# Loading keys and values as pairs with 64 KB rows, and moving the value products into the second key step

## The chip, the cores and the metric

The kernel runs on one core of a Trainium2 chip, with nothing else on the chip. The metric is the device time of one execution in microseconds; the kernel before takes 383.8 us. The profile's span is about 1.4 us shorter than the time.

Five engines work side by side: PE (matmuls), DVE (vector), ACT (activations), POOL and SP. SP issues the large loads, and at the end the one store, in a fixed order: where one load must wait, all that follow it wait too. Sixteen DMA engines move the data.

## The reference, cut to what matters

One token attends to a cache of 65536 positions; a gated mixer is computed beside it and both are blended.

```python
# Hq 32 query heads, Hkv 4 key/value heads, Sk 65536, Dh 128, D 1024, all bfloat16
q = (x @ wq)                               # wq 1024 x 4096
scores = q k^T * Dh ** -0.5                # k_cache 4 x 65536 x 128
o = softmax(scores) v                      # v_cache 4 x 65536 x 128
a = o @ wo                                 # wo 4096 x 1024
z = gelu(x @ w_in); ...; b = (z1 * g) @ w_out   # w_in 1024 x 3584, w_out 1792 x 1024
out = gate * a + (1 - gate) * b
```

There is one query position, so every byte of the caches and weights is read once for very little arithmetic. Together they are 162.0 MB.

## The kernel before

The code below is condensed; cuts are marked with dots. The caches are cut into 16 *units* of keys and 16 of values, 4 MB each: 128 partitions with a row of 32 KB (16384 bfloat16). On the chip there is room for five units: three places for keys, used in turn, and two behind them (offset `VB`) for value pairs and weights. `stream` is the list of loads in the order in which SP issues them. A load waits until the last reader of what lay in its place is done.

```python
SUB = 16384; KR = 3; VB = KR * SUB         # elements of a row; 3 key places, then 2 more

def load_k(n):  load([("k", n)], kv(A_k_cache, n), kring())          # next of the 3 places
def load_v2(n): load([("v", n), ("v", n + 1)], kv(A_v_cache, n, True), VB)

load([("wq", 0)], rows(A_wq, 0, 8), VB)
load_k(0); load_k(1)
load([("win", 0)], rows(B_w_in, 0, 8), VB)
load_k(2); load_k(3)
load([("wout", 0)], rows(B_w_out, 0, 14), VB)
for i in range(6):
    load_k(2 * i + 4); load_v2(2 * i); load_k(2 * i + 5)
load_v2(12)
# ... values 14, 15 in key places, then w_o in six pieces, the last three cut 4 + 2 + 2

def issue():
    # ... for the next load of the stream, once all that lay in its place is read:
    for c in range(0, w, SUB):             # a load of 64 KB rows goes out as two of 32 KB rows,
        m = min(SUB, w - c)                # each with its own wait and its own semaphore
        P("SP", lambda e, ...: e.dma_start(arena[:, o:o + m], src),
          w=[("slot", x) for x in grains(off + c, m)], dma="s%d" % grains(off + c, m)[0])
```

A *key step* of one unit is four transposes on DVE, each followed by eight matmuls on PE. The place of a unit is free after its fourth transpose.

```python
def k_piece(n, p):
    P("DVE", lambda e: e.transpose(ktb(i)..., sl[:, 4096 * p:4096 * (p + 1)]...),
      r=keys[2 * p:2 * p + 2], w=[("kt", i % NKT)])
    if p == 3:
        done(("k", n))                     # the place may be loaded again
    # ... 8 matmuls on PE

k_step(0)
k_step(1, evac=0, own=True)
mixer_piece()          # w_in's matmuls on PE, then a chain of some 20 small steps, most of them on DVE
k_step(2)
wout_piece()
k_step(3, evac=2)
for i in range(6):
    a = 2 * i + 4
    k_step(a, evac=a - 1, ..., pts=(2 * i, 2 * i + 1), own=True)
    pv_piece(2 * i)                        # value products of the pair
    pv_piece(2 * i + 1)
    # ...
    k_step(a + 1, late=g)
```

Of the kernel before, what the change touches and what calls it, by code (L numbers as in the profile page):

```python
# [131 lines left out]
def bass_gated_mix__gqa_block_cached__mixer_gmlp__decode_kernel(  # L132
# [19 lines left out]
    DO = A_wo.shape[1]  # L152
# [7 lines left out]
    NP = Sk // PK  # L160
# [124 lines left out]
    stream = []  # L285
    place = {}

    GRAN = 2048

    def load(keys, src, off):  # L290

        n = len(stream)
        w = src.shape[1]
        for i, key in enumerate(keys):
            place[key] = (n, off + i * (w // len(keys)), w // len(keys))
        stream.append((keys, off, src))

    def rows(w, i, c):

        return w[128 * c * i:128 * c * (i + 1), :].rearrange("(p c) n -> p (c n)", c=c)  # L300

    def kv(cache, n, both=False):

        g, u = divmod(n, NP)
        blk = cache[0, g, 2 * PK * (u // 2):2 * PK * (u // 2 + 1), :]
        if both:
            return blk.rearrange("(p x) d -> p (x d)", p=128)
        return blk.rearrange("(p h x) d -> p h (x d)", p=128, h=2)[:, u % 2, :]

    WQ_N = HQ * Dh  # L310
    VB = KR * SUB
    ring = [0]

    def kring():
        s = ring[0] % KR
        ring[0] += 1
        return s * SUB

    def load_k(n):
        load([("k", n)], kv(A_k_cache, n), kring())  # L320

    def load_v2(n):
        load([("v", n), ("v", n + 1)], kv(A_v_cache, n, True), VB)

    load([("wq", 0)], rows(A_wq, 0, 8), VB)
    load_k(0)
    load_k(1)
    load([("win", 0)], rows(B_w_in, 0, 8), VB)
    load_k(2)
    load_k(3)  # L330
    load([("wout", 0)], rows(B_w_out, 0, 14), VB)
    for i in range(6):
        load_k(2 * i + 4)
        load_v2(2 * i)
        load_k(2 * i + 5)
    load_v2(12)
    load([("v", 14)], kv(A_v_cache, 14), kring())
    load([("v", 15)], kv(A_v_cache, 15), kring())
    for i in range(3):
        load([("wo", i, 0)], rows(A_wo, i, 8), VB + 8 * DO * i)  # L340
    s3 = kring()
    for c0, c1 in [(0, 4), (4, 6), (6, 8)]:
        load([("wo", 3, c0)], rows(A_wo, 3, 8)[:, DO * c0:DO * c1], s3 + DO * c0)

    issued = [0]
    used = set()
# [2 lines left out]
    def grains(off, w):  # L349
        return list(range(off // GRAN, (off + w + GRAN - 1) // GRAN))  # L350

    def issue():

        while issued[0] < len(stream):
            n = issued[0]
            keys, off, src = stream[n]
            w = src.shape[1]
            gr = grains(off, w)
            if any(k not in used for x in gr if x in owner for k in owner[x]):
                return  # L360
            for x in gr:
                owner[x] = keys
            for c in range(0, w, SUB):
                m = min(SUB, w - c)
                P("SP", lambda e, o=OFF["RING"] + off + c, m=m, src=src[:, c:c + m]: e.dma_start(arena[:, o:o + m], src),  # L365
                  w=[("slot", x) for x in grains(off + c, m)], dma="s%d" % grains(off + c, m)[0])
            issued[0] += 1

    def use(key):
# [100 lines left out]
    def k_piece(n, p):  # L470
        if n % NP == 0 and p == 0:
            q_piece(n // NP)
        sl, keys = use(("k", n))
        i = nkt[0]
        nkt[0] += 1
        P("DVE", lambda e: e.transpose(ktb(i).bitcast(F32), sl[:, 4096 * p:4096 * (p + 1)].bitcast(F32)),  # L476
          r=keys[2 * p:2 * p + 2], w=[("kt", i % NKT)])
        if p == 3:
            done(("k", n))

        def f(e):
            for fe in range(4):
                f2, ev = fe // 2, fe % 2
                o = QP * fe + 24 - 8 * p
                for b in range(2):
                    ins = mm(e, b > 0, sc_ps(n)[:, 512 * b:512 * (b + 1)], qpad[:, o:o + 128],
                                   vw(ktb(i), 2048 * b + 64 * f2 + ev, [[128, 16], [2, 32]]),
                                   start=(p == 0 and fe == 0), stop=(p == 3 and fe == 3), skip_group_check=True)
            return ins
        P("PE", f, r=["qpad", ("kt", i % NKT)], w=[KSC(n)])  # L490

    def score_piece(n):
        P("DVE", lambda e: e.tensor_scalar(scs(n), sc_ps(n), 0.0, None, op0=ALU.add, op1=ALU.max,  # L493
                                           accum_out=maxc[:, n:n + 1]), w=[("sc", n % NSC), ("mx", n), KSC(n)])
# [18 lines left out]
    def pt_piece(n):  # L513
        P("DVE", lambda e: e.transpose(ptsb(n), psb), r=["psb"], w=[("ptsb", n % 2)])  # L514
# [17 lines left out]
    def out_first(g):  # L532
        P("DVE", lambda e: e.tensor_reduce(gcol(g, K_L), lp[:, NP * g:NP * (g + 1)], AXX, ALU.add),
          r=[("lp", NP * g + u) for u in range(NP)], w=[("l", g)])
        P("PE", lambda e: e.matmul(mb[:, 0:1], bm, gcol(g, K_L), start=True, stop=True),  # L535
          r=["bm", ("l", g)], w=["mb"])
# [84 lines left out]
    def wout_piece():  # L621
        sl, keys = use(("wout", 0))

        def f(e):
            for c in range(FC):
                j = c % 4
                for s in range(2):
                    o = DO * c + 512 * s
                    ins = mm(e, s > 0, ob[32 * j:32 * j + 1, 512 * s:512 * (s + 1)], yb[:, c:c + 1], sl[:, o:o + 512],
                             start=(c < 4), stop=(c >= FC - 4), tile_position=(0, 32 * j), skip_group_check=True)  # L630
            return ins
        P("PE", f, r=["yb"] + keys, w=["ob"])
        done(("wout", 0))
        part = scs(4)
        P("ACT", lambda e: e.activation(part[0:97, :], ob[0:97, :], ACTF.Copy), w=[("sc", 4), "ob"])

        def f(e):
            for q in range(4):
                ins = e.matmul(fb[32 * q:32 * q + 1, 0:QW], col(C_E4)[0:97, :], part[0:97, QW * q:QW * (q + 1)],
                               start=True, stop=False, tile_position=(0, 32 * q), skip_group_check=True)  # L640
            return ins
        P("PE", f, r=["e4", ("sc", 4)], w=["fb"])


    def k_step(n, evac=None, gmax=None, pts=(), own=False, late=None):

        for p in range(4):
            k_piece(n, p)
            if p == 0 and evac is not None:
                score_piece(evac)  # L650
                if gmax is not None:
                    max_first(gmax)
            if p == 1 and gmax is not None:
                max_second(gmax)
            if p == 1 and pts:
                exp_piece(pts[0])
            if p == 2 and pts:
                pt_piece(pts[0])
                exp_piece(pts[1])
            if p == 3 and pts:  # L660
                pt_piece(pts[1])
            if late is not None:
                (out_second, out_third, out_fourth, lambda g: None)[p](late)
        if own:
            score_piece(n)

    k_step(0)
    k_step(1, evac=0, own=True)
    mixer_piece()
    k_step(2)  # L670
    wout_piece()
    k_step(3, evac=2)
    for i in range(6):
        a = 2 * i + 4
        k_step(a, evac=a - 1, gmax=(a - 1) // NP if a % NP == 0 else None, pts=(2 * i, 2 * i + 1), own=True)
        pv_piece(2 * i)
        pv_piece(2 * i + 1)
        g = i // 2 if i % 2 == 1 else None
        if g is not None:
            out_first(g)  # L680
        k_step(a + 1, late=g)
    score_piece(15)
    max_first(3)
    max_second(3)
    for n in (12, 13):
        exp_piece(n)
        pt_piece(n)
    for n in (12, 13, 14, 15):
        pv_piece(n)
        if n < 14:  # L690
            exp_piece(n + 2)
            pt_piece(n + 2)
    out_first(3)
    out_second(3)
    out_third(3)
    out_fourth(3)


    for i, c0, c1 in [(0, 0, 8), (1, 0, 8), (2, 0, 8), (3, 0, 4), (3, 4, 6), (3, 6, 8)]:
        sl, keys = use(("wo", i, c0))  # L700

        def f(e, i=i, sl=sl, c0=c0, c1=c1):
            for c in range(c0, c1):
                for q in range(4):
                    o = DO * (c - c0) + QW * q
                    ins = e.matmul(fb[32 * q:32 * q + 1, 0:QW], ovec[:, 8 * i + c:8 * i + c + 1],  # L706
                                   sl[:, o:o + QW], start=False, stop=(i == 3 and c == 7),
                                   tile_position=(0, 32 * q), skip_group_check=True)
            return ins
        P("PE", f, r=[("ovec", i)] + keys, w=["fb"])  # L710
        done(("wo", i, c0))
# [34 lines left out]
```

## Time and profile before

| | before |
|---|---|
| median of 4 runs | 383.81 us (383.70 to 384.15) |
| span of the profile | 382.3 us |
| PE busy, DVE busy | 234.6 us, 211.7 us |
| DMA: share of 16 engines' time | 98.8% |

The first lines of the profile page say what bounds the kernel. "DMA" is the mean busy share of the 16 DMA engines in 40 equal slices of the span, in tenths; the line "q1" gives packets, megabytes, and the time of the packets as a share of 16 engines' span.

```profile
span 382.3 us, 2522 instructions
...
PE 234.6 (61%) x1375; PEld 56.9 (15%) x785; DVE 211.7 (55%) x229; ACT 25.3 (7%) x39; POOL 1.5 (0%) x8
...
DMA  9999999999999999999999999999999999999995
...
q1 hardware_dynamic: 6200, 162.01, 98.8%
```

The row of nines is the whole story of the kernel before: the DMA engines work from start to end, and the other engines have time to spare. The packet records of the trace give the detail: a 32 KB packet starts every 1213 ns on an engine, which is 432 GB/s for sixteen.

The second view is the timeline of SP, which shows when each load was issued (start in us, duration, engine, line, what is loaded; "x2" stands for two issues in a row, the duration then runs from the start of the first to the end of the last).

```profile
...
64.51 0.33 SPq L365 DMA_DIRECT2D arena<-in_B_w_out_dram  x1
64.88 0.43 SPq L365 DMA_DIRECT2D arena<-in_A_k_cache_dram  x1
89.59 0.81 SPq L365 DMA_DIRECT2D arena<-in_A_v_cache_dram  x2
...
309.28 8.77 SPq L365 DMA_DIRECT2D arena<-in_A_v_cache_dram  x4
...
```

Key 4 goes out at 64.88 us. The DMA engines reach it only when w_out is in, after 85 us.

The third view is the timeline of DVE around the mixer. In brackets is the time that the engine was idle before the instruction, and what ended the wait.

```profile
...
31.52 4.50 DVE L476 STREAM_TRANSPOSE arena<-arena 128x2048 f32<-128x2048 f32 x2 [0.90 <-DMA arena<-in_A_k_cache_dram]
...
64.51 1.09 DVE L588 COPY arena<-obt 128x896 f32<-128x896 f32 x1 [9.06 <-PE obt L248]
...
72.47 4.50 DVE L476 STREAM_TRANSPOSE arena<-arena 128x2048 f32<-128x2048 f32 x2
78.46 2.31 DVE L476 STREAM_TRANSPOSE arena<-arena 128x2048 f32<-128x2048 f32 x1 [1.50 <-PE scp L248]
80.93 4.51 DVE L476 STREAM_TRANSPOSE arena<-arena 128x2048 f32<-128x2048 f32 x2 [0.15 <-PE scp L248]
...
```

Key 0 starts at 31.52 us, as soon as it has landed. The mixer's chain on DVE runs from 64.51 to 72.47, then come the transposes of key 2; its fourth ends near 83.2 us.

### The profile page before, as it was taken

The numbers are of one execution on the slowest core, as the hardware profiler recorded it, in microseconds if no ns is written. First come the engines' busy times: TensorE is split into PE (matmuls) and PEld (weight loads), VectorE is DVE, ScalarE is ACT, GpSimd is POOL, SyncE is SP. The second block draws the span as 40 slices with busy tenths as digits, with TensorE's granted clock in tenths as the row PEclk, the third lists the DMA queues.
The fourth block names the chain that finished last, engine by engine and source line by source line (L and its number), as shares of the span: only waits on it lengthen the run. The fifth ranks groups of instructions, "written<-read, shape, count | busy, mean of one in ns | idle before, by whom it ended". The sixth has DMA issues, their size and how long they took to land.

```text
span 382.3 us, 2522 instructions
## 1 busy us (share of the span) xinstructions
PE 234.6 (61%) x1375; PEld 56.9 (15%) x785; DVE 211.7 (55%) x229; ACT 25.3 (7%) x39; POOL 1.5 (0%) x8
## 2 busy tenths in 40 slices
PE   0055754286687578545793777377938673849344
PEld 0011111111121111101120112012201121112121
DVE  6116952785781698067935980579448914842020
ACT  1000000102030001000210010001200100031000
POOL 1000000000000000000000000000000000000000
PEclk9996998689979599959898998786979988778695
DMA  9999999999999999999999999999999999999995
GB/s 384 439 435 425 423 417 435 439 436 433 439 425 418 432 430 439 439 432 432 429 420 429 435 439 434 429 435 426 422 432 437 435 432 429 439 425 420 423 425 220
DMA packets 6246, 162.16 MB, mean 424 GB/s; under 512 B 728, under 2 KB 732, under 8 KB 988
## 3 DMA queue, kind: packets, MB, share of 16 engines
q1 hardware_dynamic: 6200, 162.01, 98.8%
q8 instruction: 8, 0.13, 0.1%
q14 instruction: 2, 0.02, 0.0%
q10 hardware_dynamic: 36, 0.00, 0.0%
HBM read 162.01 MB, written 0.00 MB: 424 GB/s over the span
## 4 chain that ended last, share of the span: by engine, by line
DMA 61%; PE 19%; DVE 18%; SPq 1%; ACT 1%; issue 1%
DMA arena<-in_A_k_cache_dram 33%; DVE arena L476 13%; DMA arena<-in_B_w_in_dram 8%; DMA arena<-in_A_wo_dram 7%; DMA arena<-in_B_w_out_dram 6%; PE obt L246 6%; DMA arena<-in_A_wq_dram 6%; PE obt L248 5%; PE scp L246 4%; PE scp L248 4%; DVE arena L493 1%; SPq L365 1%; DVE arena L514 1%; DVE arena L464 1%; DVE arena L549 0%
## 5 line engine op out<-in xcount | busy, mean ns | idle before, releaser
L476 DVE STREAM_TRANSPOSE arena<-arena 128x2048 f32<-128x2048 f32 x64 | 145.5, 2295 | 84.5 <-DMA arena<-in_A_k_cache_dram 71.9
L246 PE MATMUL scp<-arena 128*128 128x512 bf16 x256 | 112.5, 439 | 83.4 <-DVE arena L476 61.0
L248 PE MATMUL scp<-arena 128*128 128x512 bf16 x256 | 111.0, 434 | 0.0
L246 PE MATMUL obt<-arena 128*64 128x512 bf16 (+2 forms) x334 | 64.6, 428 | 30.6 <-DMA arena<-in_A_v_cache_dram 12.4
L248 PE MATMUL obt<-arena 128*64 128x512 bf16 (+2 forms) x334 | 64.1, 424 | 0.0
L246 PEld LDWEIGHTS scp<-arena 128*128 128x128 bf16 x256 | 27.5, 107 | 192.2 <-DVE arena L476 93.8
L509 ACT ACTIVATE arena<-arena 128x1024 bf16<-128x1024 f32 x16 | 18.4, 1148 | 237.5 <-DVE arena L505 127.4
L246 PEld LDWEIGHTS obt<-arena 128*64 128x64 bf16 (+1 forms) x334 | 19.4, 116 | 86.6 <-issue 79.1
L493 DVE TENSOR_SCALAR_CACHE_REDUCE arena<-scp 128x1024 f32<-128x1024 f32 x16 | 19.3, 1205 | 9.3 <-PE scp L248 9.3
L514 DVE STREAM_TRANSPOSE arena<-arena 128x1024 bf16<-128x1024 bf16 x16 | 19.4, 1214 | 9.0 <-PE obt L248 6.4
L706 PE MATMUL fbt<-arena 128*1 128x256 bf16 x128 | 6.2, 339 | 5.9 <-DMA arena<-in_A_wo_dram 5.7
L539 DVE RECIPROCAL arena<-mbt 128x1 f32<-128x1 f32 x4 | 0.6, 139 | 14.0 <-PE mbt L535 14.0
L441 DVE CAST arena<-obt 97x1024 bf16<-97x1024 f32 x1 | 1.2, 1224 | 11.5 <-PE obt L248 11.5
L712 DVE CAST arena<-fbt 97x256 bf16<-97x256 f32 x1 | 0.4, 425 | 11.3 <-PE fbt L706 11.3
L588 DVE COPY arena<-obt 128x896 f32<-128x896 f32 x1 | 1.1, 1093 | 9.1 <-PE obt L248 9.1
L464 DVE COPY arena<-arena 32x32 bf16<-32x32 bf16 x16 | 2.7, 166 | 6.2 <-PE scp L248 6.0
L407 PE MATMUL scp<-arena 8*128 8x1 bf16 x8 | 0.6, 197 | 8.4 <-DVE arena L402 8.4
L706 PEld LDWEIGHTS fbt<-arena 128*1 128x1 bf16 x128 | 2.8, 93 | 8.8 <-DMA arena<-in_A_wo_dram 6.7
L595 ACT ACTIVATE arena<-arena 128x28 f32<-128x28 f32 x1 | 0.2, 226 | 52.4 <-DVE arena L594 52.4
L549 DVE SCALAR_TENSOR_TENSOR arena<-obt,arena 128x512 bf16<-128x512 f32 x4 | 3.0, 751 | 0.1
L601 PE MATMUL mbt<-arena 128*128 128x1 f32 x2 | 0.4, 260 | 4.3 <-DVE arena L600 4.3
L509 ACT ACTIVATION_READ_ACCUMULATOR arena<-arena 128x1 f32 x16 | 3.0, 186 | 0.0
(88 smaller groups left out, 47.0 us busy)
## 6 DMA issues: line engine op xcount, KB each, us to landing
arena<-in_A_k_cache_dram SPq DMA_DIRECT2D x16, 4096.0 KB, 38.4
arena<-in_A_v_cache_dram SPq DMA_DIRECT2D x16, 4096.0 KB, 31.1
arena<-in_A_wq_dram SPq DMA_DIRECT2D x2, 4096.0 KB, 16.8
arena<-in_A_wo_dram SPq DMA_DIRECT2D x3, 2048.0 KB, 22.6
arena<-in_B_w_in_dram SPq DMA_DIRECT2D x1, 4096.0 KB, 25.2
arena<-in_B_w_out_dram SPq DMA_DIRECT2D x1, 3584.0 KB, 23.1
arena<-in_B_w_in_dram SPq DMA_DIRECT2D x1, 3072.0 KB, 32.2
arena<-in_A_wo_dram SPq DMA_DIRECT2D x1, 1024.0 KB, 26.5
```

The lines of the kernel that those rows point to most:

```text
L246: return e.matmul(*a, **kw)
L248: one = e.matmul(*a, **kw).ins
L365: P("SP", lambda e, o=OFF["RING"] + off + c, m=m, src=src[:, c:c + m]: e.dma_start(arena[:, o:o + m], src), w=[("slot", x) for x in grains ...
L441: P("DVE", lambda e: e.tensor_copy(psb[0:97, :], ob[0:97, :]), w=["psb", "ob"])
L464: P("DVE", lambda e, pb=pb: e.tensor_copy(vw(qpad, 24 + 32 * pb, [[QP, 4], [1, 8]], 32 * pb, 32), vw(qall, 8 * g, [[32, 4], [1, 8]], 32 * ...
L476: P("DVE", lambda e: e.transpose(ktb(i).bitcast(F32), sl[:, 4096 * p:4096 * (p + 1)].bitcast(F32)), r=keys[2 * p:2 * p + 2], w=[("kt", i % ...
L493: P("DVE", lambda e: e.tensor_scalar(scs(n), sc_ps(n), 0.0, None, op0=ALU.add, op1=ALU.max, accum_out=maxc[:, n:n + 1]), w=[("sc", n % NSC ...
L509: P("ACT", lambda e: e.activation(psb, scs(n), ACTF.Exp, bias=gcol(n // NP, K_NB), scale=SCALE, accum_out=lp[:, n:n + 1]), r=[("sc", n % N ...
L514: P("DVE", lambda e: e.transpose(ptsb(n), psb), r=["psb"], w=[("ptsb", n % 2)])
L549: P("DVE", lambda e: e.scalar_tensor_tensor(osc, ob[:, 512:1024], gcol(g, K_FB), osc, op0=ALU.mult, op1=ALU.add), r=[("fh", g, 1), "psb"], ...
L588: P("DVE", lambda e: e.tensor_copy(vw(zr, 0, [[FB4, 2], [32, FC], [1, 32]]), vw(ob, 0, [[512, 2], [1, FC], [FC, 32]])), w=[KZR, "ob"])
L706: ins = e.matmul(fb[32 * q:32 * q + 1, 0:QW], ovec[:, 8 * i + c:8 * i + c + 1], sl[:, o:o + QW], start=False, stop=(i == 3 and c == 7), ti ...
```

## The change

The intent is fewer and longer packets. Where two units that lie side by side in the cache can also lie side by side on the chip, they are loaded as one load with rows of 64 KB. Keys now come in pairs where the three places allow it, and stream and places are laid out for that: the last values move to other places, and so does w_o. A load is no longer cut into two. The value products run inside the second key step, since all values of a pair now land at once. The last cut of w_o is finer (5 + 2 + 1 instead of 4 + 2 + 2).

```diff
-    GRAN = 2048
+    GRAN = 1024
...
+    def load_k2(n, slot):
+        load([("k", n), ("k", n + 1)], kv(A_k_cache, n, True), slot * SUB)
...
     load([("wq", 0)], rows(A_wq, 0, 8), VB)
-    load_k(0)
-    load_k(1)
+    load_k2(0, 0)
     load([("win", 0)], rows(B_w_in, 0, 8), VB)
-    load_k(2)
-    load_k(3)
+    load_k(2, 2)
+    load_k(3, 0)
     load([("wout", 0)], rows(B_w_out, 0, 14), VB)
     for i in range(6):
-        load_k(2 * i + 4)
-        load_v2(2 * i)
-        load_k(2 * i + 5)
-    load_v2(12)
-    load([("v", 14)], kv(A_v_cache, 14), kring())
-    load([("v", 15)], kv(A_v_cache, 15), kring())
+        a = 2 * i + 4
+        if i % 3 == 2:
+            load_k(a, 2)
+            load_k(a + 1, 0)
+        else:
+            load_k2(a, (1, 0)[i % 3])
+        load_v2(2 * i, VB)
+    load_v2(12, SUB)
+    load([("v", 14)], kv(A_v_cache, 14), VB)
+    load([("v", 15)], kv(A_v_cache, 15), VB + SUB)
...
-            for c in range(0, w, SUB):
-                m = min(SUB, w - c)
-                P("SP", ... one load of 32 KB rows, w=[("slot", x) for x in grains(off + c, m)], ...)
+            P("SP", lambda e, o=OFF["RING"] + off, w=w, src=src: e.dma_start(arena[:, o:o + w], src),
+              w=[("slot", x) for x in gr], dma="s%d" % gr[0])
...
     mixer_piece()
     k_step(2)
-    wout_piece()
     k_step(3, evac=2)
+    wout_piece()
     for i in range(6):
-        k_step(a, evac=a - 1, ..., pts=(2 * i, 2 * i + 1), own=True)
-        pv_piece(2 * i)
-        pv_piece(2 * i + 1)
-        k_step(a + 1, late=g)
+        k_step(a, evac=a - 1, ..., pts=(2 * i, 2 * i + 1))
+        k_step(a + 1, evac=a, mid=mid)     # mid: both pv_piece, between the 2nd and 3rd transpose
```

More of the change, by code (lines that the diff above doesn't have):

```diff
@@ L311, in bass_gated_mix__gqa_block_cached__mixer_gmlp__decode_kernel, with load_k, load_v2 @@
     VB = KR * SUB
-    ring = [0]
-    def kring():
-        s = ring[0] % KR
-        ring[0] += 1
-        return s * SUB
-    def load_k(n):
-        load([("k", n)], kv(A_k_cache, n), kring())
-    def load_v2(n):
-        load([("v", n), ("v", n + 1)], kv(A_v_cache, n, True), VB)
+    def load_k(n, slot):
+        load([("k", n)], kv(A_k_cache, n), slot * SUB)
+    def load_k2(n, slot):
+        load([("k", n), ("k", n + 1)], kv(A_k_cache, n, True), slot * SUB)
+    def load_v2(n, off):
+        load([("v", n), ("v", n + 1)], kv(A_v_cache, n, True), off)
     load([("wq", 0)], rows(A_wq, 0, 8), VB)
-    load_k(0)
-    load_k(1)
+    load_k2(0, 0)
     load([("win", 0)], rows(B_w_in, 0, 8), VB)
-    load_k(2)
-    load_k(3)
+    load_k(2, 2)
+    load_k(3, 0)
     load([("wout", 0)], rows(B_w_out, 0, 14), VB)
     for i in range(6):
-        load_k(2 * i + 4)
-        load_v2(2 * i)
-        load_k(2 * i + 5)
-    load_v2(12)
-    load([("v", 14)], kv(A_v_cache, 14), kring())
-    load([("v", 15)], kv(A_v_cache, 15), kring())
+        a = 2 * i + 4
[8 more added lines that the diff above has]
+    load([("v", 15)], kv(A_v_cache, 15), VB + SUB)
+    WO_AT = [0, 8 * DO, 16 * DO, 24 * DO]
+    WO_CUT = [(0, 5), (5, 7), (7, 8)]
     for i in range(3):
-        load([("wo", i, 0)], rows(A_wo, i, 8), VB + 8 * DO * i)
-    s3 = kring()
-    for c0, c1 in [(0, 4), (4, 6), (6, 8)]:
-        load([("wo", 3, c0)], rows(A_wo, 3, 8)[:, DO * c0:DO * c1], s3 + DO * c0)
+        load([("wo", i, 0)], rows(A_wo, i, 8), WO_AT[i])
+    for c0, c1 in WO_CUT:
+        load([("wo", 3, c0)], rows(A_wo, 3, 8)[:, DO * c0:DO * c1], WO_AT[3] + DO * c0)
     issued = [0]
@@ L362, in issue @@
                 owner[x] = keys
-            for c in range(0, w, SUB):
-                m = min(SUB, w - c)
-                P("SP", lambda e, o=OFF["RING"] + off + c, m=m, src=src[:, c:c + m]: e.dma_start(arena[:, o:o + m], src),
-                  w=[("slot", x) for x in grains(off + c, m)], dma="s%d" % grains(off + c, m)[0])
+            P("SP", lambda e, o=OFF["RING"] + off, w=w, src=src: e.dma_start(arena[:, o:o + w], src),
+              w=[("slot", x) for x in gr], dma="s%d" % gr[0])
             issued[0] += 1
@@ L476, in k_piece @@
         P("DVE", lambda e: e.transpose(ktb(i).bitcast(F32), sl[:, 4096 * p:4096 * (p + 1)].bitcast(F32)),
-          r=keys[2 * p:2 * p + 2], w=[("kt", i % NKT)])
+          r=keys[4 * p:4 * p + 4], w=[("kt", i % NKT)])
         if p == 3:
@@ L642, in wout_piece, with k_step @@
         P("PE", f, r=["e4", ("sc", 4)], w=["fb"])
-    def k_step(n, evac=None, gmax=None, pts=(), own=False, late=None):
+    def k_step(n, evac=None, gmax=None, pts=(), own=False, mid=None):
         for p in range(4):
@@ L661, in k_step, with out_rest @@
                 pt_piece(pts[1])
-            if late is not None:
-                (out_second, out_third, out_fourth, lambda g: None)[p](late)
+            if p == 1 and mid is not None:
+                mid()
         if own:
             score_piece(n)
+    def out_rest(g):
+        out_second(g)
+        out_third(g)
+        out_fourth(g)
     k_step(0)
@@ L670, in bass_gated_mix__gqa_block_cached__mixer_gmlp__decode_kernel, with mid @@
     k_step(2)
+    k_step(3, evac=2)
     wout_piece()
-    k_step(3, evac=2)
     for i in range(6):
         a = 2 * i + 4
-        k_step(a, evac=a - 1, gmax=(a - 1) // NP if a % NP == 0 else None, pts=(2 * i, 2 * i + 1), own=True)
-        pv_piece(2 * i)
-        pv_piece(2 * i + 1)
         g = i // 2 if i % 2 == 1 else None
-        if g is not None:
-            out_first(g)
-        k_step(a + 1, late=g)
-    score_piece(15)
-    max_first(3)
-    max_second(3)
-    for n in (12, 13):
-        exp_piece(n)
-        pt_piece(n)
+        k_step(a, evac=a - 1, gmax=(a - 1) // NP if a % NP == 0 else None, pts=(2 * i, 2 * i + 1))
+        if i == 5:
+            k_step(a + 1, evac=a, own=True, mid=lambda: pv_piece(10))
+            max_first(3)
+            max_second(3)
+            exp_piece(12)
+            pv_piece(11)
+            out_first(2)
+            pt_piece(12)
+            out_rest(2)
+            continue
+        def mid(i=i, g=g):
+            pv_piece(2 * i)
+            pv_piece(2 * i + 1)
+            if g is not None:
+                out_first(g)
+        k_step(a + 1, evac=a, mid=mid)
+        if g is not None:
+            out_rest(g)
+    exp_piece(13)
+    pt_piece(13)
     for n in (12, 13, 14, 15):
@@ L693, in bass_gated_mix__gqa_block_cached__mixer_gmlp__decode_kernel @@
     out_first(3)
-    out_second(3)
-    out_third(3)
-    out_fourth(3)
-    for i, c0, c1 in [(0, 0, 8), (1, 0, 8), (2, 0, 8), (3, 0, 4), (3, 4, 6), (3, 6, 8)]:
+    out_rest(3)
+    for i, c0, c1 in [(0, 0, 8), (1, 0, 8), (2, 0, 8)] + [(3, c0, c1) for c0, c1 in WO_CUT]:
         sl, keys = use(("wo", i, c0))
```

## The prediction

> **What bounds the kernel now.** The transfers from HBM. On the profile page the DMA row is at 9 in 39 of 40 slices; queue q1 keeps the 16 DMA engines busy for 98.8% of the 382.3 us span; PE is 61% and DVE 55% busy. The Trainium skill ("DMA: Bandwidth & Descriptors", Specifications) gives a fabric ceiling of 435 GB/s; the trace agrees: 32 KB packets start every 1213 ns on an engine, 432 GB/s for 16. The packet records show no stretch with dry engines before the end. Engines finish at 377.0 to 379.1 us; the late ones because each carried one 16 KB instruction fetch (queue q8, 8 of them), which costs about 1.5 us. So compute that moves is worth nothing, unless a load is issued too late.
>
> **What it removes.** In 14 places (5 key pairs, 7 value pairs, wq, w_in) two rows of up to 32 KB become one. From the periods (1213 ns for 32 KB, 611 for 16 KB) a packet costs about 8.5 ns beyond its bytes, a semaphore packet 6 ns. Each pair saves an engine 8 x 8.5 + 6 = 74 ns, together 1.0 us, if a 64 KB row goes as one packet. The last w_o piece halves: about 0.2 us of 0.63 us of final matmuls. At most 1.2 us, 0.3%, all on the critical path.
>
> **What it adds.** Coarser hand-offs: an 8 MB load waits until both its places are free, and nothing of it is usable before all has landed. I followed the hand-offs with durations of the trace (transpose 2.3 us, full key step 12.0, two value products 7.1, 8 MB in 19.4). In the steady part margins are 4 us or more: the next key pair is issued about 12 us after a pair lands, while 19.4 us of values load. The exception is the first pair after the weights, keys 4 and 5. Before, key 4 needed only key 1's place and was issued at 64.9 us. Now it needs key 2's too. Keys 0 and 1 land together, so key 0 starts near 41.2 instead of 31.5, key 1's matmuls end near 63.8 instead of 54.2, the mixer's near 67.0 instead of 64.3, its 8 us DVE chain near 75.1, and key 2's transposes, with slow first matmuls (430 ns) as before, near 85.8 instead of 83.2. The queue runs dry when w_out is in, at 85.0 to 85.3 us on most engines. From issue to first packet took 1.0 us at the start, and the first packets 1.8 us instead of 1.2. So I expect one gap of about 2 us on most engines near 86 us: more than the saving.
>
> **Predicted time:** 384.3 us, 8 in 10 between 382.6 and 386.0. Faster by over 2%: 0.01; within 2%: 0.97; slower by over 2%: 0.02.
>
> **What would show it.** Packets of 64 KB, near 2418 ns apart: right; of 32 KB: no saving. The issue of keys 4 and 5 near 86 us: right; before 84: no gap. The DMA share by stretches clearly below 1 between 84 and 90 us, and nowhere else before the end. DVE and PE busy time within 2%; DMA bytes 162.0 MB, unchanged.
>
> **What would make it wrong.** Key 2's transposes done 2 us earlier: then 382.7. A second starved hand-off, most likely a key pair that waits for a key step which an instruction fetch delayed: 386 or more. Long rows that run slower than short ones.

## More of the kernel before

(Four small loads of 2 KB or less are issued by ACT, on a queue of their own.)

## The result, and the profile after

| | before | after |
|---|---|---|
| median of 4 runs | 383.81 us | 384.43 us (383.91 to 385.37) |
| ratio | | 1.0017 (95%: 1.0003 to 1.0032) |
| span of the profile | 382.3 us | 383.5 us |
| DMA: packets of q1 | 6200 | 4184 |
| DMA: share of 16 engines' time | 98.8% | 98.2% |

A ratio is the mean time of one kernel's fast runs over the mean of the other's in the same rounds, so it is not quite the ratio of the medians quoted beside it. The kernel became 0.17% slower. The interval is only just clear of 1: it allows 0.1 to 1.2 us.

The same lines of the page, after:

```profile
span 383.5 us, 2499 instructions
...
PE 224.8 (59%) x1375; PEld 55.5 (14%) x785; DVE 210.7 (55%) x229; ACT 25.3 (7%) x39; POOL 1.5 (0%) x8
...
DMA  9999999989999999989999999999999999999995
...
q1 hardware_dynamic: 4184, 162.01, 98.2%
```

The megabytes are the same in a third fewer packets. The first 8 in the DMA row is the ninth slice, 76.7 to 86.3 us, just where the prediction looks for a gap. (In the slice of the other 8, 163 to 173 us, the packet records show no dry engine.) SP's timeline, after:

```profile
...
67.22 0.33 SPq L364 DMA_DIRECT2D arena<-in_B_w_out_dram  x1
86.26 0.33 SPq L364 DMA_DIRECT2D arena<-in_A_k_cache_dram  x1
99.98 0.33 SPq L364 DMA_DIRECT2D arena<-in_A_v_cache_dram  x1
121.36 0.33 SPq L364 DMA_DIRECT2D arena<-in_A_k_cache_dram  x1
...
292.22 44.95 SPq L364 DMA_DIRECT2D arena<-in_A_v_cache_dram  x4
...
```

The first key pair of the loop goes out at 86.26 us; key 4 went out at 64.88 before. DVE's timeline says why:

```profile
...
41.33 4.50 DVE L475 STREAM_TRANSPOSE arena<-arena 128x2048 f32<-128x2048 f32 x2 [8.55 <-DMA arena<-in_A_k_cache_dram]
...
67.23 1.09 DVE L587 COPY arena<-obt 128x896 f32<-128x896 f32 x1 [1.92 <-PE obt L248]
...
75.38 4.50 DVE L475 STREAM_TRANSPOSE arena<-arena 128x2048 f32<-128x2048 f32 x2
81.38 2.31 DVE L475 STREAM_TRANSPOSE arena<-arena 128x2048 f32<-128x2048 f32 x1 [1.50 <-PE scp L248]
83.92 4.51 DVE L475 STREAM_TRANSPOSE arena<-arena 128x2048 f32<-128x2048 f32 x2 [0.23 <-PE scp L248]
...
```

Key 0 starts 9.8 us later, since it lands together with key 1; the mixer starts 2.7 us later, and key 2's fourth transpose (the first of the two that start at 83.92) ends at 86.2. The chain of waits goes over exactly these steps (start, us, what):

```profile
...
83.92 2.32 DVE arena L475
86.26 22.91 DMA arena<-in_A_k_cache_dram
109.19 2.32 DVE arena L475
```

What it did to the DMA engines is in the view by stretches. A row gives the stretch and its length; busy time and count of PE, PEld, DVE, ACT and POOL; then the granted PE clock, the DMA share and GB/s. A packet is counted whole in the stretch in which it starts, so a share can come out over 1, and shares of short stretches are rough. First before, then after, from 84 to 90 us:

```profile
84.00:90.00 6.00, 3.10 (x34) 0.54 (x16) 4.78 (x4) 0.41 (x1) 0.00 (x0) 1.00 0.99 425
```

```profile
84.00:90.00 6.00, 5.08 (x23) 1.02 (x11) 6.00 (x5) 0.00 (x0) 0.00 (x0) 1.00 0.71 261
```

The share falls from 0.99 to 0.71. By the packet records, 13 of the 16 engines finished w_out by 85.5 us and got the first keys at 87.2 to 88.0: 1.9 us idle on the mean of the 16. The first packets after the gap then took about 3.1 us (2.57 to 3.32) instead of 2.42, another 0.6 us. Packets of the size of 64 KB start every 2414 to 2418 ns, against 2 x 1213 = 2426 in the kernel before.

### The profile page after: what moved, and what is told of

The parts are those of the page before. It is cut to its first block, busy times and chain, and to the rows that moved or that the text cites. A ratio compares the mean times of both kernels' runs of the same rounds, so it can differ in the third digit from the quotient of the medians.

```text
span 383.5 us, 2499 instructions
## 1 busy us (share of the span) xinstructions
PE 224.8 (59%) x1375; PEld 55.5 (14%) x785; DVE 210.7 (55%) x229; ACT 25.3 (7%) x39; POOL 1.5 (0%) x8
## 3 DMA queue, kind: packets, MB, share of 16 engines
q1 hardware_dynamic: 4184, 162.01, 98.2%
## 4 chain that ended last, share of the span: by engine, by line
DMA 57%; DVE 24%; PE 18%; issue 1%; SPq 0%; ACT 0%; DVEq 0%
DMA arena<-in_A_k_cache_dram 39%; DVE arena L475 18%; DMA arena<-in_A_v_cache_dram 10%; DMA arena<-in_A_wo_dram 8%; PE scp L246 6%; PE scp L248 5%; PE obt L246 3%; PE obt L248 3%; DVE arena L513 2%; DVE arena L492 1%; PE fbt L718 1%; DVE arena L589 0%; DVE arena L587 0%; PE mbt L500 0%; SPq L364 0%
## 5 line engine op out<-in xcount | busy, mean ns | idle before, releaser
L246 PE MATMUL scp<-arena 128*128 128x512 bf16 x256 | 106.7, 417 | 94.1 <-DVE arena L475 91.2
L248 PE MATMUL scp<-arena 128*128 128x512 bf16 x256 | 106.1, 414 | 0.0
L246 PE MATMUL obt<-arena 128*64 128x512 bf16 (+2 forms) x334 | 63.1, 421 | 22.1 <-DMA arena<-in_A_v_cache_dram 22.1
L248 PE MATMUL obt<-arena 128*64 128x512 bf16 (+2 forms) x334 | 62.4, 417 | 0.0
L246 PEld LDWEIGHTS scp<-arena 128*128 128x128 bf16 x256 | 26.5, 104 | 195.9 <-DVE arena L475 121.0
L246 PEld LDWEIGHTS obt<-arena 128*64 128x64 bf16 (+1 forms) x334 | 18.3, 113 | 76.9 <-issue 59.0
L513 DVE STREAM_TRANSPOSE arena<-arena 128x1024 bf16<-128x1024 bf16 x16 | 19.4, 1213 | 8.9 <-PE obt L248 6.4
L553 PE MATMUL mbt<-arena 128*128 128x128 bf16 x16 | 2.0, 262 | 4.7 <-DVE arena L548 4.7
L559 DVE TENSOR_TENSOR arena<-mbt,arena 128x128 f32<-128x128 f32 x4 | 1.2, 291 | 4.4 <-PE mbt L553 4.4
```

What stands on the lines that cost most here:

```text
L246: return e.matmul(*a, **kw)
L248: one = e.matmul(*a, **kw).ins
L513: P("DVE", lambda e: e.transpose(ptsb(n), psb), r=["psb"], w=[("ptsb", n % 2)])
L553: ins = e.matmul(mb[:, 0:128], sel[:, 128 * c:128 * (c + 1)], osc[:, 128 * c:128 * (c + 1)], start=(c == 0), stop=(c == 3))
L559: P("DVE", lambda e: e.tensor_tensor(vw(ot, 0, [[8, 16], [1, 8]]), vw(mb, 0, [[8, 16], [1, 8]]), vw(mq, 0, [[1, 16], [0, 8]]), ALU.mult), ...
```

## The experiments

Two questions were open. Is the gap near 86 us what the kernel paid, or is it absorbed later? And are the long rows worth what was put down for them? The theory was: rows save about 1 us, the gap costs about 2. The rivals were: the gap is absorbed, because late engines set the end anyway; or long rows are worth nothing. Every run below was correct, timed in 5 rounds. Names that begin with a are edits of the kernel after, names with b of the kernel before. The ratio is always to the kernel before, in the same job.

| run | median us | ratio (95%) |
|---|---|---|
| after | 384.43 | 1.0017 (1.0003 to 1.0032) |
| a1_split45 | 382.54 | 0.9967 (0.9955 to 0.9980) |
| a2_split01 | 382.77 | 0.9976 (0.9964 to 0.9989) |
| a3_mixer_late | 382.66 | 0.9969 (0.9955 to 0.9982) |
| a4_short_rows | 400.94 | 1.0447 (1.0422 to 1.0472) |
| a5_short_rows2 | 385.78 | 1.0053 (1.0040 to 1.0065) |
| a6_late_short | 383.92 | 1.0002 (0.9990 to 1.0015) |
| a7_delay | 386.75 | 1.0077 (1.0064 to 1.0090) |
| b2_delay | 383.85 | 1.0001 (0.9987 to 1.0014) |
| b1_long_rows | 386.32 | 1.0068 (1.0054 to 1.0081) |
| b3_long_rows2 | 383.30 | 0.9989 (0.9976 to 1.0003) |
| a8_pv_after | 382.42 | 0.9965 (0.9953 to 0.9978) |
| a9_old_cut | 382.90 | 0.9977 (0.9964 to 0.9989) |

### Three ways to close the gap

The gap has three links, and each of three edits cuts another one. In the first, key 4 needs key 1's place alone:

```diff
+        if i == 0:
+            load_k(a, 1)
+            load_k(a + 1, 2)
-        if i % 3 == 2:
+        elif i % 3 == 2:
```

> After, with keys 4 and 5 as two loads of 32 KB rows, in the same two places. Key 4 then needs only key 1's place. Theory (the late issue of the pair 4,5 leaves the queue dry near 86 us and costs 1.9 us of idle engines plus about 0.6 us of slow first packets): key 4 is issued near 67 us, no dry stretch near 86 us, and the time falls by 2.4 us from 384.4 to 382.0 (one pair less costs 0.1). Rival (the gap is absorbed, because the end is set by the engines that carry an instruction fetch or because long rows run slower later on): 384.2 to 384.6, as after.

Measured: key 4 was issued at 66.9 us, no stretch was dry (0.03 us of idle time before the end), and the time was 382.54 us.

```profile
66.89 18.65 SPq L367 DMA_DIRECT2D arena<-in_A_k_cache_dram  x2
```

In the second, keys 0 and 1 land one by one:

```diff
-    load_k2(0, 0)
+    load_k(0, 0)
+    load_k(1, 1)
```

> After, with keys 0 and 1 as two loads; the pair 4,5 stays a pair. Theory (keys 0 and 1 landing together starts key 0 at 41.3 instead of 31.5 us and delays key 2 by 3 us): key 0 starts near 31.5, the pair is issued near 83.3 us, 2 us before w_out is in, the dry stretch shrinks to 0 to 0.3 us, time 382.0 to 382.4. Rival (the pair's two places alone matter, the landing does not): the issue stays near 86 us and the time near 384.4.

Measured: the pair was issued at 83.87 us instead of 86.26. By the packet records 0.14 us of idle time was left, and the time was 382.77 us, 0.4 over the expected range's upper end.

```profile
83.87 0.33 SPq L365 DMA_DIRECT2D arena<-in_A_k_cache_dram  x1
```

In the third, all pairs stay, and the mixer's arithmetic leaves the way of key 2:

```diff
         P("PE", f, r=["xT"] + keys, w=["ob"])
         done(("win", 0))
+
+    def mixer_rest():
         NZ = 2 * FB4
...
     mixer_piece()
     k_step(2)
+    mixer_rest()
```

> After, with all pairs kept, and the mixer's arithmetic on DVE (8 us) moved behind key step 2; its matmuls stay where they were, so w_in's place comes free as before. Theory: key 2's transposes end near 78.5 us, the pair 4,5 is issued then, 7 us ahead, no gap, time 381.9. Rival (gap absorbed): 384.4. If the moved arithmetic makes a new wait (w_out's matmuls later), that shows as a late issue of the first values, expected near 100 us as in after.

Measured: 382.66 us. SP's timeline of this run has the pair 6 us earlier, and its stretch is full again:

```profile
67.32 0.33 SPq L364 DMA_DIRECT2D arena<-in_B_w_out_dram  x1
79.86 0.33 SPq L364 DMA_DIRECT2D arena<-in_A_k_cache_dram  x1
```

```profile
84.00:90.00 6.00, 0.91 (x5) 0.68 (x5) 4.57 (x13) 0.42 (x2) 0.00 (x0) 0.70 1.01 436
```

Three different edits with nothing else in common give 382.5 to 382.8 us. The rival that the gap is absorbed is out. The gap cost 1.8 us: the ratio of after over that of a3 is 1.0017 / 0.9969 = 1.0048, times 383.8. The two intervals together leave about 0.8 us to either side, since the four runs of after alone spread over 1.5 us. The expected 2.4 us was higher, but it is inside that, so whether all of the idle time and of the slow first packets was paid is not shown.

### Making the gap longer

One more transpose on DVE between the mixer and key step 2, in the kernel after and, as a control, in the kernel before (the same edit, with the slice of keys as it stands there):

```diff
     mixer_piece()
+    P("DVE", lambda e: e.transpose(ktb(0).bitcast(F32), ktb(1).bitcast(F32)), r=[("kt", 1)], w=[("kt", 0), "delay"])
     k_step(2)
...
-          r=keys[4 * p:4 * p + 4], w=[("kt", i % NKT)])
+          r=keys[4 * p:4 * p + 4] + ["delay"], w=[("kt", i % NKT)])
```

> After, with one more transpose of 2.3 us on DVE between the mixer and key step 2; nothing reads its result. Theory: key 2, the issue of the pair 4,5 (86.3 to 88.6 us) and the end all move by 2.3 us: 386.7. Rival (later slack takes up a gap): less than half of it, under 385.6.

> Before, with the same extra transpose of 2.3 us between the mixer and key step 2. Theory: before, no load waits for key 2 soon after it (key 4 needs key 1's place, issued at 64.9 us), so nothing moves: 383.7 to 384.0. If the extra work costs time by itself, 386.

Measured: the kernel after rises by 2.3 us, to 386.75, again with about 0.8 us to either side; the kernel before does not move (383.85 beside 383.68), though its key 2 starts later too. The pair's issue moved to 88.08 us, 1.8 us later and not 2.3, since all had started some 0.5 us earlier in this execution (w_out was issued at 66.67 instead of 67.22). By the packet records the idle time rose from 1.9 to 3.6 us. The stretch from 84 to 92 us fell to a share of 0.54:

```profile
88.08 0.33 SPq L364 DMA_DIRECT2D arena<-in_A_k_cache_dram  x1
```

```profile
84.00:92.00 8.00, 7.10 (x31) 1.39 (x14) 7.79 (x6) 0.00 (x0) 0.00 (x0) 0.96 0.54 196
```

So one and the same piece of DVE work costs about its full length in one kernel and nothing in the other. In these two kernels its cost depends on whether the issue of a load that is due hangs on it.

### What a long row is worth

The first try at short rows with hand-offs as coarse as in after was a miss. Its edit cut every long load in two and had each use wait for both halves, but did so by recording each key's transposes as *readers* of the whole pair:

```diff
-            P("SP", ... one load, w=[("slot", x) for x in gr], ...)
+            before = [x for g in gr for x in R.readers.get(("slot", g), ())]
+            for c in range(0, w, SUB):
+                ...
+                d = P("SP", ... 32 KB rows, w=[("slot", x) for x in g2], ...)
+                d.deps += [(x, False) for x in before if ...]
...
+        def __getitem__(self, i):                       # the grains that a transpose reads:
+            return list.__getitem__(self, i) + self.rest   # its own, and the other half's
```

> After, with every load of rows over 32 KB issued as two loads of 32 KB rows, one behind the other, each waiting for all of the pair's place, and every use waiting for both: hand-offs as coarse as in after, rows as short as in before. Theory (a 64 KB row saves about 12 ns against two of 32 KB, by the periods 2414 and 1213 ns; 14 x 8 rows, and 6 ns for each semaphore packet): the gap near 86 us stays, the saving goes, time 384.4 + 1.5 = 385.9. Rival (long rows give nothing, or slow spells eat it): 384.4 or less.

Measured: 400.94 us. The first key's place was now held until the second key was transposed too. The next key pair went out at 132.32 us instead of 121.36, and the stretch from 120 to 140 us had a share of 0.65:

```profile
120.00:140.00 20.00, 15.85 (x103) 3.75 (x52) 12.30 (x8) 1.57 (x4) 0.00 (x0) 1.00 0.65 266
```

A second such stretch lay near 250 us. By the packet records these two left the engines idle for 7.0 and 6.3 us; with the gap near 86 us, which was still there, and 0.6 us near 355 it was 15.3 us in all. The run says nothing about row length, but it shows how near the steady part is to the same trouble: the issue at 121.36 leads by about 5 us, and 11 us of delay brought 7.0 us of idle engines.

The mended edit waits for both halves to land and reads its own part only:

```diff
-                      w=[("slot", x) for x in g2], ...)
+                      w=[("slot", x) for x in g2] + [("landed", n, c)], ...)
...
+            return list.__getitem__(self, i) + self.whole   # whole: ("landed", n, c) of both halves
```

> The previous try at short rows made places come free later, because each key's transposes were recorded as readers of the whole pair; here they wait for the whole pair to land but are readers of their own key alone. Everything else as in after. Theory (long rows save about 12 ns for each 64 KB): the issues stand as in after (the pair 4,5 near 86 us), the dry stretch stays near 1.6 us, no other dry stretch, time 384.4 + 1.2 to 1.5 = 385.6 to 385.9. Rival (row length gives nothing, the gain over before of the three mended kernels comes from something else): 384.4.

Measured: 385.78 us. The pair 4,5 was issued at 85.66 us, so the gap was there as in after, with 1.4 us of idle time by the packet records (1.9 in after), and nothing else was dry. Then the same short rows together with the mended mixer:

> The mixer's arithmetic behind key step 2 (no gap), and all rows 32 KB as before, hand-offs as coarse as in after. Theory: without gap and without long rows nothing is left of the change but the last cut: 382.66 + 1.3 = 383.9, the time of before or 0.2 less. Rival (row length gives nothing): 382.7.

Measured: 383.92 us beside 383.88 of before. With neither gap nor long rows, nothing measurable is left of the change. This run also holds the parts that no run undoes one by one: the new places of w_o and of the last values, and w_out's matmuls behind key step 3 instead of before it. The long rows are worth 383.92 - 382.66 = 1.26 us without a gap and 385.78 - 384.43 = 1.35 us with one (medians of different jobs; about 0.7 us to either side by the ratios, whose intervals do not overlap in either pair). A small part of it is the second load's own semaphore packets, 6 ns each in the trace.

### Long rows in the order of before

```diff
-            for c in range(0, w, SUB):
-                m = min(SUB, w - c)
-                P("SP", ... 32 KB rows ...)
+            P("SP", lambda e, o=OFF["RING"] + off, w=w, src=src: e.dma_start(arena[:, o:o + w], src),
+              w=[("slot", x) for x in gr], dma="s%d" % gr[0])
```

> Before, with loads of more than 32 KB a row issued whole: wq, w_in and the 7 value pairs as rows of 64 (56) KB, the keys one by one as they were, order of work unchanged. Theory: 9 of the 14 savings, no gap (key 4 still needs key 1's place alone): 383.86 - 0.9 = 382.9 to 383.1. Rival (coarser value hand-offs cost a gap too): at or over 383.9, with a dry stretch before a value pair.

Measured: 386.32 us; the expectation failed and the rival's sign was there. Values 12 and 13 as one load wait for both value places and go out at 319.57 us, where value 12 alone went at 309.28. SP's timeline and the stretch:

```profile
319.57 1.28 SPq L363 DMA_DIRECT2D arena<-in_A_v_cache_dram  x3
```

```profile
316.00:322.00 6.00, 3.84 (x36) 1.09 (x16) 1.43 (x1) 0.00 (x0) 0.00 (x0) 1.00 0.87 328
```

The packet records show about half of the engines dry from 318.2 us on and all of them by 320.2; packets start again at 320.5. The idle time is 2.0 us on the mean. The kernel after does not have this one: it puts values 12 and 13 into key places and issues them at 305.33 us. To test that this one hand-off was the cause, it alone was undone:

```diff
-    load_v2(12)
+    load([("v", 12)], kv(A_v_cache, 12), VB)
+    load([("v", 13)], kv(A_v_cache, 13), VB + SUB)
```

> The run of long rows alone in the order of before missed: its last pair of values (12 and 13) waited until both value places were free, was issued at 319.6 instead of 309.3 us, and left the queue dry for 2.0 us near 320. Here values 12 and 13 are two loads again, in the same places, so that value 12 needs value 10's place alone; 8 long loads stay. Theory (the miss was that one hand-off): value 12 is issued near 316 us or before, no dry stretch over 0.3 us, time 383.0 to 383.3 (8 savings of about 0.1 us). Rival (long rows do not pay in the order of before, whatever the hand-off): 383.7 or more.

Measured: value 12 was issued at 316.76 us, 0.08 us of idle time was left, and the median was 383.30 us (four runs from 383.18 to 383.75, one of 385.00).

```profile
316.76 4.75 SPq L364 DMA_DIRECT2D arena<-in_A_v_cache_dram  x4
```

The 3 us came back, so the hand-off was the cause. The gain over before, 0.1%, has an interval that touches 1, so whether long rows pay in this order is not shown by this run alone.

### The other parts of the change

The value products after the second key step instead of inside it, on a3_mixer_late:

```diff
-        k_step(a + 1, evac=a, mid=mid)
+        k_step(a + 1, evac=a)
+        mid()
...
-            k_step(a + 1, evac=a, own=True, mid=lambda: pv_piece(10))
+            k_step(a + 1, evac=a, own=True)
+            pv_piece(10)
```

> The kernel without gap (mixer's arithmetic behind key step 2), with the value products after the second key step instead of inside it: that part of the change undone. Theory (compute that moves is worth nothing while loads are issued ahead): the issues of values move by about 5 us later and still lead by more than 5 us: 382.5 to 382.9, as without it. If the move inside was needed, dry stretches before value pairs and 383.5 or more.

Measured: 382.42 us, ratio 0.9965, beside 0.9969 with the products inside. The issues of values moved by 0 to 4.4 us, and nothing was dry. This part of the change is worth nothing that can be measured. It was tried on the mended kernel alone, not on the kernel after as it stands.

The old cut of w_o, also on a3_mixer_late:

```diff
-    WO_CUT = [(0, 5), (5, 7), (7, 8)]
+    WO_CUT = [(0, 4), (4, 6), (6, 8)]
```

> The kernel without gap, with the old cut of the last w_o part (4, 2 and 2 rows of weights instead of 5, 2 and 1). Theory: the last piece has 8 matmuls instead of 4 after it lands: 0.2 us more, 382.85. If it makes no difference, 382.66.

Measured: 382.90 us, ratio 0.9977. That is 0.2 to 0.3 us more than a3, as expected in size, but the intervals overlap: it is not shown.

Kernels a1, a3 and a8 beat the kernel before by 0.3% and the kernel after by 0.5%; a2 and a9 beat them by 0.2% and 0.4%.

## Why the prediction was right

The time, 384.43 us, lies 0.1 us from the predicted 384.3 and well inside the range. That it came so near is luck: the runs of after spread over 1.5 us, and the interval of the ratio allows 0.1 to 1.2 us. What was right is the reasoning. Point by point:

- **The bound.** Right. The DMA row of nines, and the control: 2.3 us of DVE work added to the kernel before cost nothing.
- **The gap.** Right in place, cause and size. Predicted: key 0 near 41.2 us, the mixer's matmuls end near 67.0, key 2's transposes near 85.8, a gap of about 2 us on most engines. Measured: 41.33, 67.2, 86.2, and 1.9 us. Cutting any one of its three links gave the time back, and lengthening it cost about its length.
- **The saving of long rows.** Right in kind: 1.0 us predicted, 1.26 to 1.35 measured, with 1.0 inside the intervals. The term was 8.5 ns for a packet; two packets of 32 KB take 2426 ns and one of 64 KB 2414 to 2418, a difference of 8 to 12. For 8 packets in each of 14 loads that is 0.9 to 1.3 us.
- **The last cut of w_o.** Predicted 0.2 us; 0.2 to 0.3 seen, not separated from zero.
- **The sum.** Before to a3 is -1.2 us (ratio 0.9969), a3 to after is +1.8, together +0.6. This only splits the measured change, since the 1.8 was taken from the same two ratios. The check from outside is a6: with neither gap nor long rows the time is that of before.
- **No other gap.** Right for the kernel after: no other stretch is dry before the end. a4 and b1 show that this was no matter of course, since one coarser hand-off made each of them dry elsewhere. b1 also shows the limit of the reasoning: the same walk through the hand-offs missed the one of values 12 and 13.
- **PE and DVE busy within 2%.** DVE yes (210.7 and 211.7 us). PE fell by 4%, from 234.6 to 224.8 us, with the same 1375 instructions; the mean of a key matmul went from 439 to 417 ns. The granted clock was no higher (0.848 after, 0.854 before), and why the mean fell is not shown. The 10 us of busy time went without any gain in the kernel's time, so it was a poor sign to choose.

## What to carry to other kernels

In a kernel that is bound by its loads, cost a change by two sums first: what it saves on each packet, and for each load the time between its issue and the moment the queue runs out. A larger load waits for the last of the places that it covers and is usable only when all of it has landed; follow both delays through to the next issue, above all where the steady order begins and where it ends. When a long load opens a gap, splitting that one load or moving unrelated work off its chain keeps the gain of all others.

## What the Trainium skill lacked or had wrong

- "DMA: Bandwidth & Descriptors", Rules for kernel authors and Bandwidth: they advise 128 partitions and at least 1 MiB for a load, and a load of 4 MB is far beyond that. The page names a fixed overhead of some 3 cycles for each packet (Bandwidth, "Why small descriptors are slow"), but works it out for 256 bytes alone; no figure there compares 32 KB rows with 64 KB rows. Here two rows of 32 KB took 2426 ns on an engine and one of 64 KB 2414 to 2418; over 14 such loads the long rows were worth 1.3 us of 384 (a6 against a3).
- "Perfetto Trace Analysis", DMA Optimizations: it says that smaller loads may start sooner, but a shorter whole it offers only for the case "If DMA engines are generally idle". Here they were busy for 98% of the span, and splitting one load (a1_split45) still gained 1.9 us, because it moved an issue from 86.3 to 66.9 us.
- "Runtime: NRT & Kernel Launch", Instruction fetch mechanics: it says that instructions are fetched in 16 KiB blocks and that the cost is mostly hidden. The blocks agree (8 packets of 16384 bytes on q8). In the kernel before, on busy DMA engines, they are not hidden there: each took 1.0 to 1.1 us of one engine, and beside seven of the eight a packet took 1.68 to 1.76 us instead of 1.21. Half of the engines finished near 377.1 us, and the others some 1.5 us later. That the late ones are those that served a fetch is inferred from their number and from the spread of the engines, which rose from 0.5 to 1.9 us at the first fetch; no run takes the fetches away, so what they cost the kernel is not shown. In the profiled run of b3_long_rows2 (385.0 us) the spread of the engines rose from 1.9 to 3.4 us at the seventh fetch. It may have met an engine that had already served one; the records carry no engine numbers, so this stays open.
- No page has the price of a dry queue beyond the idle time. The first 64 KB packets after the gap took about 3.1 us instead of 2.42, and those at the start of the kernel about 3.0. The nearest figure is the first-byte latency of this path, about 0.6 us ("DMA: Bandwidth & Descriptors", Specifications); whether the added 0.6 us is the same thing no run shows.
- "DMA: Bandwidth & Descriptors", Queues, rings and completion order: an engine takes turns between queues at whole packets, typically of 9 to 17 descriptors. The trace agrees on the turns, but a turn of the long loads was a single row: in the kernel after, packets of the small loads started at 16.20, 18.62 and 21.04 us, one 64 KB row (2.42 us) apart. It also shows a price. The 2-byte load of b_sp, the last of the small loads on that other queue, landed behind several such rows: the matmul that waits for it ran at 13.39 us before and at 21.77 after. It was harmless here, as w_in's issue moved from 27.2 to 29.4 us and was not due before 40 us, when keys 0 and 1 were in. First the line of PE's timeline before, then after:

```profile
13.39 0.16 PE L412 MATMUL mbt<-arena 1*128 1x2 bf16 x1 [4.34 <-DMA arena<-in_B_b_sp_dram]
```

```profile
21.77 0.16 PE L411 MATMUL mbt<-arena 1*128 1x2 bf16 x1 [10.22 <-DMA arena<-in_B_b_sp_dram]
```
